# Scores of three attention units in one TensorE block instead of two, with PV written into the unit's own score banks

## Chip, cores and metric

The kernel runs on one core of a Trainium2 chip. The metric is the device time of one launch, in microseconds (us). The engines are TensorE (PE in the profile, with its weight loads as PEld), VectorE (DVE), ScalarE (ACT), GpSimd (POOL) and SyncE (SP). PE writes only into PSUM, which has eight banks; ACT and DVE read it from there.

## What is computed

Sliding-window attention with a linear bias, followed by a feed-forward layer whose gate is h times cos(h):

```python
scores = q @ k.T / sqrt(64)                       # q, k, v: 8 batches, 8 heads, 576 rows, 64 wide
scores = where((rel >= 0) & (rel < 128), scores - slope[h] * rel, -1e9)
x = softmax(scores) @ v                           # brought to 4608 rows x 512
h = x @ w_in                                      # 512 -> 2048
out = (h * cos(h)) @ w_out                        # 2048 -> 512, float32
```

## The kernel before

**Tiling.** The 4608 rows of x are nine chunks of 512 rows (`c` in the main loop). Attention is cut into units of 128 query rows, eight per batch: `units(b)` gives (b, 0, 0), which has all eight heads of the first 128 rows; then for qb = 1, 2, 3 two units each with four heads (hh = 0, 1); then (b, 4, 0), the tail of 64 rows with all eight heads. Because the window is 128 wide, a block of queries needs only its own block of keys and the one before it.

**One unit** goes through these steps:

- scores (L540, matmul in L559): 16 matmuls for the tail, 8 for any other unit. Each uses 64 of PE's 128 rows; the two heads of a pair use the two halves of the rows and write two banks.
- exps (L582): one ACT instruction over both banks (128x1024), from PSUM to the tile `p`.
- mask (L591): one DVE multiplication of `p` by `exp(bias)`, which is 0 outside the window.
- pv (L608): matmuls of `p` with v, 65 columns wide (the 65th is the row sum); 8 matmuls, or 16 for the tail. A unit with qb 0 or 4 is wide and writes both banks 2 and 3; any other writes one of them.
- norm (L648): a DVE reciprocal of the row sum into `rec` and one multiplication, or two for a wide unit, into an SBUF tile.
- the way into `xT`: either a DMA transpose on SP's queue (`x_dma`), or two or four PE transposes and a copy by ACT or DVE (`x_pe`), which use the same bank as the PV.

**Feed-forward.** `moe1(c)` makes for each of 16 column blocks four matmuls 512 wide into one bank (L750), a Sin on ACT (L755) and a product on DVE (L759). `moe2(c)` makes for each of four row blocks 16 matmuls 512 wide (L803), a copy to SBUF by ACT or DVE (L810, L811) and a store on SP.

**Banks.** `SB` = 4 to 7 hold scores, `UB` = 2, 3 hold PV, `OB` = 0, 1 hold moe2's sums. moe1 goes round the banks 2 to 7.

**Order.** The main loop lists for each chunk c: moe1(c), then the attention units that the next chunk needs (phase c: eight units, nine in phase 6), then moe2(c). Before it stands phase -1, seven units. `attention` takes the units two at a time: one block of scores for two units, two exps, two masks, then PV of both together, or one after the other where a wide unit is among them. The listed operations then go through `Plan.schedule`: a list scheduler with a fixed cost for each operation and a priority (norm and the way into xT first, then exps, masks and PV, then scores, moe1, moe2). It writes one fixed order for each engine, and `Plan.emit` sets the semaphore waits. The ACT table allows only Exp of phase c, then Sin of chunk c + 1, and so on in turn. Nothing of the order is decided on the chip; an instruction that is not ready holds up all behind it on its engine.

The first four units of a phase (two in phase 0) go into xT through SP's queue ahead of everything that depends on them: the DMA transposes of the next batch's q and k (L406, L409) stand behind them on SP, and the loads of v on POOL's queue wait for them.

Of the kernel before, what the change touches and what calls it, by code (L numbers as in the profile page):

```python
# [8 lines left out]
F32 = mybir.dt.float32  # L9
BF16 = mybir.dt.bfloat16  # L10
# [274 lines left out]
def bass_alibi_sliding__then__act_gcu_kernel(  # L285
# [8 lines left out]
    with ExitStack() as ctx:  # L294
# [26 lines left out]
        cosb = [sb(f"cos{i}", [128, 512], F32) for i in range(NCOS)]  # L321
        NOB = 4
        ob = [sb(f"ob{i}", [128, 512], F32) for i in range(NOB)]
        rec = [sb(f"rec{i}", [128, 8], F32) for i in range(2)]
        ident = sb("ident", [128, 128])
        zeros = sb("zeros", [128, 128])
        halfpi = sb("halfpi", [128, 1], F32)
# [2 lines left out]

        ps = ctx.enter_context(nc.psum_tensor("ps", [128, 8, 512], F32))
        BPE = 2
        QUOTA = [8, 8, 8, 8, 8, 8, 9]
        BIASED = [(0, 0, 0)] + [(0, qb, hh) for qb in range(1, 3) for hh in range(2)]
        SB, UB, OB = [4, 5, 6, 7], [2, 3], [0, 1]
# [204 lines left out]
        def scores(us, slot):  # L540

            def f(e):
                ins = None
                for n, u in enumerate(us, slot):
                    b, qb, hh = u
                    banks = SB[2 * n:2 * n + 2]
                    acc = u in BIASED
                    if qb == 0:
                        jobs = [(128 * pr, 128, pr, 0) for pr in range(NPAIR)]
                    elif qb == 4:  # L550
                        jobs = [(128 * pr + 64 * i, 64, pr, 3 + i) for pr in range(NPAIR)
                                for i in range(2)]
                    else:
                        jobs = [(256 * i + 128 * j, 128, 2 * hh + i, qb - 1 + j)
                                for i in range(2) for j in range(2)]
                    for n, (c0, n_, pr, kc) in enumerate(jobs):
                        stop = not acc or n == len(jobs) - 1
                        for x in range(2):
                            ins = e.matmul(ps[:, banks[x], c0:c0 + n_], keys_ap(b, x, pr, kc),  # L559
                                           query_ap(b, x, pr, qb, n_), start=not acc, stop=stop)  # L560
                return ins
            keys, held, occ = [], [], 0
            for n, u in enumerate(us, slot):
                keys += tkeys(u)
                held += [("B", x) for x in SB[2 * n:2 * n + 2]]
                occ += 250 if u[1] == 4 else 230
                if u in BIASED:
                    b, qb, hh = u
                    for x in range(2):
                        rhs = BT[:, x, :, 128:256] if qb == 0 else BT[:, x, 2 * hh:2 * hh + 2, :]  # L570
                        prs = range(NPAIR) if qb == 0 else range(2 * hh, 2 * hh + 2)
                        bank = SB[2 * n + x]
                        op("pe", lambda e, rhs=rhs, bank=bank: e.matmul(  # L573
                            ps[:, bank, :], ident[:, :], rhs, start=True, stop=False),
                           r=[("BT", 2 * pr + x) for pr in prs] + ["ident"], w=[("B", bank)],
                           occ=216, lat=379, pri=2)
            op("pe", f, r=keys, w=held, occ=occ, lat=occ + 165, mode=1, pri=2)
# [2 lines left out]
        pbuf = {}  # L580

        def exps(u, n, table):  # L582
            banks = SB[2 * n:2 * n + 2]
            i = pbuf[u] = pcount[0] % NP
            pcount[0] += 1
            op("act", lambda e: e.activation(  # L586
                P[i][:, 0:1024], ps[:, banks[0]:banks[0] + 2, :].rearrange("p a b -> p (a b)"),
                ACTF.Exp, scale=0.125),
               w=[("B", x) for x in banks] + [("P", i)], occ=940, lat=1040, table=table, pri=1)
# [18 lines left out]
        def pv(us):  # L608

            def f(e):  # L610
                ins = None
                for u, ub in us:
                    b, qb, hh = u
                    i, V = pbuf[u], vp[b % 2]
                    if qb in (0, 4):
                        for x in range(2):
                            for k_ in range(NPAIR):
                                h = 2 * k_ + x
                                o = ps[:, UB[x], 65 * k_:65 * k_ + 65]
                                c0 = 512 * x + 128 * k_  # L620
                                ins = e.matmul(o, P[i][:, c0:c0 + 128],  # L621
                                               V[:, 3 if qb else 0, h, 0:65],
                                               start=True, stop=not qb)
                                if qb:
                                    ins = e.matmul(o, P[i][:, c0 + 64:c0 + 192], V[:, 4, h, 0:65],  # L625
                                                   start=False, stop=True)
                        continue
# [11 lines left out]
            for u, ub in us:  # L639
                b, qb, hh = u  # L640
                wide = qb in (0, 4)
                reads += [("P", pbuf[u]), ("vinit", b % 2)]
                reads += [("v", b % 2, t) for t in range(max(0, qb - 1), qb + 1)]
                held += [("B", x) for x in (UB if wide else [ub])]
                occ += 480 if qb == 4 else 240
            op("pe", f, r=reads, w=held, pri=1, occ=occ, lat=occ + 165)

        def norm(u, ub, n):  # L648
            b, qb, hh = u
            rc = rec[n % 2]  # L650
            if qb in (0, 4):
                m = 64 if qb else 128
                xt_ = xtl[b % 2] if qb else xfirst
                key = ("xtl", b % 2) if qb else "xfirst"
                U = ps[0:m, UB[0]:UB[0] + 2, 0:260].rearrange("p x (k c) -> p x k c", c=65)
                rv = rc[0:m, 0:8].rearrange("p (x k) -> p x k", x=2)
                o = xt_[:, :].rearrange("p (k x d) -> p x k d", k=4, x=2)
                op("dve", lambda e: e.reciprocal(rv, U[:, :, :, 64]),
                   w=[("B", UB[0]), ("B", UB[1]), ("rec", n % 2)], occ=120, lat=200, pri=0)
                for x in range(2):  # L660
                    op("dve", lambda e, x=x: e.tensor_tensor(
                        o[:, x, :, :], U[:, x, :, 0:64],
                        rv[:, x, :, None].broadcast_to([m, 4, 64]), ALU.mult),
                       r=[("rec", n % 2)], w=[("B", UB[x]), key], occ=340, lat=420, pri=0)
                return
            U = ps[:, ub, 0:260].rearrange("p (r x c) -> p r x c", r=2, c=65)
            rv = rc[:, 0:4].rearrange("p (r x) -> p r x", r=2)
            key = ("xnat", n % NX)
            o = xnat[n % NX][:, :].rearrange("p (r x d) -> p r x d", r=2, x=2)
            op("dve", lambda e: e.reciprocal(rv, U[:, :, :, 64]),  # L670
               w=[("B", ub), ("rec", n % 2)], occ=100, lat=182, pri=0)
            op("dve", lambda e: e.tensor_tensor(  # L672
                o, U[:, :, :, 0:64], rv[:, :, :, None].broadcast_to([128, 2, 2, 64]), ALU.mult),
               r=[("rec", n % 2)], w=[("B", ub), key], occ=340, lat=425, pri=0)

        def xkeys(prs, t0, n):
            return [("xT", pr, t // 64) for pr in prs for t in range(t0, t0 + n, 64)]
# [1 line left out]
        def x_pe(u, ub, n):  # L679
# [3 lines left out]
            if qb in (0, 4):  # L683
                m = 64 if qb else 128
                xt_ = xtl[b % 2] if qb else xfirst
                rk = [("xtl", b % 2) if qb else "xfirst"]
                half = ps[:, UB[0]:UB[0] + 2, :].bitcast(BF16)[:, :, 768:1024]

                def f(e):
                    ins = None  # L690
# [2 lines left out]
                        ins = e.transpose(half[:, y, c0:c0 + m],  # L693
                                          xt_[:, 128 * k_:128 * k_ + 128], ident[0:m, 0:m])
                    return ins
                banks = UB[0:1] if qb else UB
                op("pe", f, r=rk + ["ident"], w=[("B", x) for x in banks],
                   occ=240, lat=410, pri=0)
                if qb:
                    parts = [(xT[:, :, t0:t0 + 64],  # L700
                              half[:, 0, :].rearrange("p (k t) -> p k t", k=4), every, [UB[0]])]
                else:
                    parts = [(xT[:, 2 * y:2 * y + 2, t0:t0 + 128],
                              half[:, y, :].rearrange("p (k t) -> p k t", k=2),
                              range(2 * y, 2 * y + 2), [UB[y]]) for y in range(2)]
            else:
                dst = ps[:, ub, :].bitcast(BF16)[:, 768:1024]

# [111 lines left out]

        def attention(us, phase):

            begin = []
            for g in range(0, len(us), 2):
                two = us[g:g + 2]
                if phase < 0:
                    for n, u in enumerate(two):
                        scores([u], n)
                        exps(u, n, 0)
                        mask(u)  # L830
                else:
                    scores(two, 0)
                    for n, u in enumerate(two):
                        exps(u, n, 2 * phase + 2)
                    for u in two:
                        mask(u)
                sets = [list(zip(two, UB))]
                if phase < 0 or any(u[1] in (0, 4) for u in two):
                    sets = [[s] for s in sets[0]]
                for set_ in sets:  # L840
                    pv(set_)
                    after = []
                    for u, ub in set_:
                        n = ucount[0]
                        ucount[0] += 1
                        norm(u, ub, n)
                        soon = g < (4 if phase else 2) and phase >= 0
                        after.append((soon, t_first(u) // CH > phase + 1, u, ub, n))
                    for soon, late, u, ub, n in after:
                        if soon:  # L850
# [2 lines left out]
                            x_dma(u, n)  # L853
                        else:
                            x_pe(u, ub, n)
            return begin

        load_qk("q", q, 0, 0)
# [95 lines left out]
```

## Time and profile before

| what | value |
|---|---|
| median of 3 runs | 311.3 us (311.07 to 311.45) |
| the profiled execution | 311.13 us |
| its span, first to last instruction | 309.3 us |
| busy PE, ACT, DVE, POOL | 301.1, 205.6, 189.9, 97.2 us |
| granted PE clock | 1.000 |
| PE matmuls L803, L750 | 130.7 us, 112.4 us |

In a row of the timeline stand the start (us from the start of the span), the time from the start of the first to the end of the last of the merged instructions, the engine, the line, the operation, output and input, and the count. In square brackets stands how long the engine had been idle before it, and what ended that. In the chain of work that ended last, a piece is a start, a length and what ran. Matmuls overlap: one that is shown with 0.38 us is followed by the next after 0.216 us. A few per cent of the matmul records are missing, so a merged row can show one less than ran.

### The profile page before, as it was taken

To read this page: it belongs to the slowest core of one execution; us is meant where nothing else is said; L and a number is where in the kernel's file an instruction comes from. 1 tells how busy PE (TensorE), PEld (TensorE's weight loads), DVE (VectorE), ACT (ScalarE), POOL (GpSimd) and SP (SyncE) were. 2 spreads that over 40 slices of the span, in tenths; PEclk is the share of its full clock that TensorE was granted. 3 is DMA by queue.
4 is the path that set the end of the run, shared out by engine and by line. 5 is a ranking of instruction groups with operands and counts; after the bars stand their busy time and mean duration, and the time that the engine had idled before them with its cause. 6 is when DMAs were issued, how large, how long until landed. Compare 5 with 4: busy or idle time off the path is not lost.

```text
span 309.3 us, 6639 instructions
## 1 busy us (share of the span) xinstructions
PE 301.1 (97%) x2675; PEld 161.4 (52%) x2717; DVE 189.9 (61%) x400; ACT 205.6 (66%) x276; POOL 97.2 (31%) x122
## 2 busy tenths in 40 slices
PE   7899999999999999999999999999999999999996
PEld 5689756445544554455445544454455544444444
DVE  6687667585867586857784777487748880453000
ACT  7797865885787778758777768668668682462211
POOL 8997200582055505550573056405000000000000
PEclk9999999999999999999999999999999999999999
DMA  9999999999499949994999399949923201101112
GB/s 147 172 204 207 207 163 195 184 159 144 77 130 141 194 84 146 131 202 109 151 142 189 89 116 159 194 118 158 117 94 77 45 0 36 68 0 69 69 70 100
DMA packets 150334, 39.09 MB, mean 126 GB/s; under 512 B 138913, under 2 KB 145313, under 8 KB 150305
## 3 DMA queue, kind: packets, MB, share of 16 engines
q0 software_dynamic: 100688, 18.10, 84.1%
q1 hardware_dynamic: 49344, 20.33, 31.7%
q8 instruction: 21, 0.34, 0.5%
q10 hardware_dynamic: 272, 0.26, 0.3%
q14 instruction: 9, 0.07, 0.1%
HBM read 36.70 MB, written 9.44 MB: 149 GB/s over the span
## 4 chain that ended last, share of the span: by engine, by line
PE 96%; issue 1%; DVE 1%; ACT 1%; POOL 0%; ACTq 0%; POOLq 0%
PE ps L803 40%; PE ps L750 35%; PE ps L559 6%; PE ps L775 5%; PE ps L633 2%; PE ps L635 2%; PE ps L500 2%; PE ps L621 2%; PE ps L573 1%; PE ps L712 1%; PE ps L625 1%; DVE gT L759 0%; ACT cos L755 0%; ACT p L586 0%; PE ps L495 0%
## 5 line engine op out<-in xcount | busy, mean ns | idle before, releaser
L803 PE MATMUL ps<-w_outb,gT 128*128 128x512 bf16 (+2 forms) x563 | 130.7, 373 | 2.1 <-issue 1.0
L750 PE MATMUL ps<-xT,w_inb 128*128 128x512 bf16 x501 | 112.4, 379 | 0.6
L759 DVE TENSOR_TENSOR gT<-ps,cos 128x512 bf16<-128x512 f32 x128 | 86.0, 689 | 38.4 <-ACT cos L755 22.0
L755 ACT ACTIVATE cos<-ps,halfpi 128x512 f32<-128x512 f32 x128 | 85.7, 687 | 25.9 <-PE ps L750 17.9
L803 PEld LDWEIGHTS ps<-w_outb,gT 128*128 128x128 bf16 x592 | 53.4, 98 | 56.8 <-DVE ob L811 0.2
L750 PEld LDWEIGHTS ps<-xT,w_inb 128*128 128x128 bf16 x512 | 49.5, 98 | 59.2 <-issue 1.1
L586 ACT ACTIVATE p<-ps 128x1024 bf16<-128x1024 f32 x64 | 62.1, 1021 | 27.1 <-PE ps L559 26.8
L386 POOL DMA_DIRECT2D vp<-in_v_dram x40 | 33.9, 870 | 84.8 <-DMA xT<-xnat 63.4
L605 DVE TENSOR_TENSOR p<-p,emask 128x1024 bf16<-128x1024 bf16 x59 | 40.0, 685 | 21.3 <-ACT p L586 21.3
L810 ACT ACTIVATE ob<-ps 128x512 f32<-128x512 f32 (+2 forms) x26 | 15.1, 581 | 38.5 <-PE ps L803 38.4
L397 POOL DMA_DIRECT2D qnat<-in_q_dram x30 | 25.3, 872 | 19.1 <-DMA qt<-qnat 19.1
L397 POOL DMA_DIRECT2D knat<-in_k_dram x30 | 25.4, 878 | 11.8 <-DMA kt<-knat 10.1
L559 PE MATMUL ps<-qt,kt 64*128 64x128 bf16 (+1 forms) x576 | 20.8, 213 | 0.3 <-DVE kt L516 0.3
L559 PEld LDWEIGHTS ps<-qt,kt 64*128 64x128 bf16 x576 | 14.7, 95 | 10.9 <-ACT p L586 5.5
L672 DVE TENSOR_TENSOR xnat<-ps,rec 128x256 bf16<-128x256 f32 x48 | 18.3, 419 | 0.2
L775 PE MATMUL ps<-xT,w_inb 128*128 128x128 bf16 x256 | 16.4, 219 | 0.0
L633 PEld LDWEIGHTS ps<-vp,p 128*128 128x128 bf16 x192 | 13.0, 97 | 6.1 <-issue 5.9
L633 PE MATMUL ps<-vp,p 128*128 128x65 bf16 x192 | 15.0, 193 | 0.2 <-DVE xT L722 0.2
L635 PE MATMUL ps<-vp,p 128*128 128x65 bf16 x192 | 15.1, 193 | 0.0
L775 PEld LDWEIGHTS ps<-xT,w_inb 128*128 128x128 bf16 x256 | 14.6, 98 | 0.7
L635 PEld LDWEIGHTS ps<-vp,p 128*128 128x128 bf16 x192 | 12.5, 97 | 0.1
L811 DVE COPY ob<-ps 128x512 f32<-128x512 f32 x11 | 7.5, 682 | 8.1 <-PE ps L803 8.1
(66 smaller groups left out, 157.3 us busy)
## 6 DMA issues: line engine op xcount, KB each, us to landing
out_dram<-ob SPq DMA_DIRECT2D x35, 256.0 KB, 3.2
vp<-in_v_dram POOLq DMA_DIRECT2D x32, 128.0 KB, 6.6
qnat<-in_q_dram POOLq DMA_DIRECT2D x24, 128.0 KB, 6.9
knat<-in_k_dram POOLq DMA_DIRECT2D x24, 128.0 KB, 5.4
w_outb<-in_moe_w_out_dram POOLq DMA_DIRECT2D x4, 512.0 KB, 21.1
w_inb<-in_moe_w_in_dram POOLq DMA_DIRECT2D x3, 512.0 KB, 11.1
qrows<-in_q_dram POOLq DMA_DIRECT2D x1, 576.0 KB, 14.4
krows<-in_k_dram POOLq DMA_DIRECT2D x1, 576.0 KB, 16.8
```

The source lines that it names most:

```text
L386: op("pool", [lambda e, t=t, rows=rows: e.dma_start(vp[b % 2][0:rows, t, :, 0:64], v[b, :, 128 * t:128 * t + rows, :].rearrange("h p d -> ...
L397: fns.append(lambda e, t=t, rows=rows: e.dma_start(nat[which][0:rows, t, :, :], src[b, :, 128 * t:128 * t + rows, :].rearrange("h p d -> p ...
L559: ins = e.matmul(ps[:, banks[x], c0:c0 + n_], keys_ap(b, x, pr, kc), query_ap(b, x, pr, qb, n_), start=not acc, stop=stop)
L586: op("act", lambda e: e.activation(P[i][:, 0:1024], ps[:, banks[0]:banks[0] + 2, :].rearrange("p a b -> p (a b)"), ACTF.Exp, scale=0.125), ...
L605: op("dve", lambda e: e.tensor_tensor(p, p, m, ALU.mult), r=[("P", i), ("EM", 0), ("EM", 1)], w=[("P", i)], occ=600, lat=690, pri=1)
L633: e.matmul(o, P[i][:, c0:c0 + 128], V[:, qb - 1, h, 0:65], start=True, stop=False)
L635: ins = e.matmul(o, P[i][:, c0 + 128:c0 + 256], V[:, qb, h, 0:65], start=False, stop=True)
L750: op("pe", lambda e, kc=kc: e.matmul(ps[:, bank, :], w_in[:, kc, 128 * fc:128 * fc + 128], xT[:, kc, r0:r0 + CH], start=(kc == 0), stop=(k ...
L755: op("act", lambda e: e.activation(cosb[ci][:, :], ps[:, bank, :], ACTF.Sin, bias=halfpi[:, 0:1]), r=["halfpi"], w=[("B", bank), ("cos", c ...
L759: op("dve", lambda e: e.tensor_tensor(gT[gi][:, fc, :], ps[:, bank, :], cosb[ci][:, :], ALU.mult), r=[("cos", ci)], w=[("B", bank)] + [("g ...
L775: ins = e.matmul(ps[:, bank, 128 * i:128 * i + 128], w_in[:, kc, 128 * fc:128 * fc + 128], xT[:, kc, t0:t0 + 128], start=(kc == 0), stop=( ...
L803: op("pe", lambda e, t=t, fc=fc, bank=bank, j0=j0, j1=j1: e.matmul(ps[:, bank, 0:j1 - j0], gT[gi][:, fc, 128 * t:128 * t + 128], w_out[:, ...
```

## The change

From phase 1 on the units are grouped by three: 3, 3, 2 in phases 1 to 5, and 3, 3, 3 in phase 6. The scores of a group are one block on PE. Unit n of a group has the banks 4 and 5, 6 and 7, or 2 and 3 (`SLOT`), for its scores, its PV and its transposes. Each unit's mask, PV and norm are listed unit by unit. Phases -1 and 0 stay in groups of two with the old banks. There are four `rec` tiles instead of two.

```diff
-        rec = [sb(f"rec{i}", [128, 8], F32) for i in range(2)]
+        rec = [sb(f"rec{i}", [128, 8], F32) for i in range(4)]
...
+        GROUPS = [[2] * 4] + [[3, 3, 2]] * 5 + [[3] * 3]
+        SLOT = [4, 6, 2]
@@ scores @@
-                    banks = SB[2 * n:2 * n + 2]
+                    banks = [SLOT[n], SLOT[n] + 1]
@@ exps @@
-            banks = SB[2 * n:2 * n + 2]
+            banks = [SLOT[n], SLOT[n] + 1]
@@ pv, the wide unit @@
-                                o = ps[:, UB[x], 65 * k_:65 * k_ + 65]
+                                o = ps[:, ub + x, 65 * k_:65 * k_ + 65]
...
-                held += [("B", x) for x in (UB if wide else [ub])]
+                held += [("B", x) for x in ([ub, ub + 1] if wide else [ub])]
@@ attention @@
-            begin = []
-            for g in range(0, len(us), 2):
-                two = us[g:g + 2]
+            begin, g = [], 0
+            sizes = ([[2] * 4] + GROUPS + [[], []])[phase + 1]
+            own = 3 in sizes
+            for many in sizes:
+                some = us[g:g + many]
                 if phase < 0:
...
                 else:
-                    scores(two, 0)
-                    for n, u in enumerate(two):
+                    scores(some, 0)
+                    for n, u in enumerate(some):
                         exps(u, n, 2 * phase + 2)
-                    for u in two:
+                if not own:
+                    outs = [UB[0] if u[1] in (0, 4) else UB[n] for n, u in enumerate(some)]
+                    for u in some if phase >= 0 else []:
                         mask(u)
-                sets = [list(zip(two, UB))]
-                if phase < 0 or any(u[1] in (0, 4) for u in two):
-                    sets = [[s] for s in sets[0]]
+                    sets = [list(zip(some, outs))]
+                    if phase < 0 or any(u[1] in (0, 4) for u in some):
+                        sets = [[x] for x in sets[0]]
+                else:
+                    sets = [[x] for x in zip(some, SLOT)]
                 for set_ in sets:
+                    if own:
+                        mask(set_[0][0])
                     pv(set_)
...
-                        soon = g < (4 if phase else 2) and phase >= 0
+                        soon = us.index(u) < (4 if phase else 2) and phase >= 0
...
+                g += many
```

The norm and the transposes of a wide unit follow the same exchange, from `UB[0]`, `UB[1]` to `ub`, `ub + 1`.

More of the change, by code (lines that the diff above doesn't have):

```diff
@@ L564, in scores @@
                 keys += tkeys(u)
-                held += [("B", x) for x in SB[2 * n:2 * n + 2]]
+                held += [("B", SLOT[n] + x) for x in range(2)]
                 occ += 250 if u[1] == 4 else 230
@@ L571, in scores @@
                         prs = range(NPAIR) if qb == 0 else range(2 * hh, 2 * hh + 2)
-                        bank = SB[2 * n + x]
+                        bank = SLOT[n] + x
                         op("pe", lambda e, rhs=rhs, bank=bank: e.matmul(
@@ L649, in norm @@
             b, qb, hh = u
-            rc = rec[n % 2]
+            rc = rec[n % 4]
             if qb in (0, 4):
@@ L654, in norm @@
                 key = ("xtl", b % 2) if qb else "xfirst"
-                U = ps[0:m, UB[0]:UB[0] + 2, 0:260].rearrange("p x (k c) -> p x k c", c=65)
+                U = ps[0:m, ub:ub + 2, 0:260].rearrange("p x (k c) -> p x k c", c=65)
                 rv = rc[0:m, 0:8].rearrange("p (x k) -> p x k", x=2)
@@ L658, in norm @@
                 op("dve", lambda e: e.reciprocal(rv, U[:, :, :, 64]),
-                   w=[("B", UB[0]), ("B", UB[1]), ("rec", n % 2)], occ=120, lat=200, pri=0)
+                   w=[("B", ub), ("B", ub + 1), ("rec", n % 4)], occ=120, lat=200, pri=0)
                 for x in range(2):
@@ L663, in norm @@
                         rv[:, x, :, None].broadcast_to([m, 4, 64]), ALU.mult),
-                       r=[("rec", n % 2)], w=[("B", UB[x]), key], occ=340, lat=420, pri=0)
+                       r=[("rec", n % 4)], w=[("B", ub + x), key], occ=340, lat=420, pri=0)
                 return
@@ L670, in norm @@
             op("dve", lambda e: e.reciprocal(rv, U[:, :, :, 64]),
-               w=[("B", ub), ("rec", n % 2)], occ=100, lat=182, pri=0)
+               w=[("B", ub), ("rec", n % 4)], occ=100, lat=182, pri=0)
             op("dve", lambda e: e.tensor_tensor(
                 o, U[:, :, :, 0:64], rv[:, :, :, None].broadcast_to([128, 2, 2, 64]), ALU.mult),
-               r=[("rec", n % 2)], w=[("B", ub), key], occ=340, lat=425, pri=0)
+               r=[("rec", n % 4)], w=[("B", ub), key], occ=340, lat=425, pri=0)
         def xkeys(prs, t0, n):
@@ L686, in x_pe @@
                 rk = [("xtl", b % 2) if qb else "xfirst"]
-                half = ps[:, UB[0]:UB[0] + 2, :].bitcast(BF16)[:, :, 768:1024]
+                half = ps[:, ub:ub + 2, :].bitcast(BF16)[:, :, 768:1024]
                 def f(e):
@@ L695, in f @@
                     return ins
-                banks = UB[0:1] if qb else UB
+                banks = [ub] if qb else [ub, ub + 1]
                 op("pe", f, r=rk + ["ident"], w=[("B", x) for x in banks],
@@ L700, in x_pe @@
                     parts = [(xT[:, :, t0:t0 + 64],
-                              half[:, 0, :].rearrange("p (k t) -> p k t", k=4), every, [UB[0]])]
+                              half[:, 0, :].rearrange("p (k t) -> p k t", k=4), every, [ub])]
                 else:
@@ L704, in x_pe @@
                               half[:, y, :].rearrange("p (k t) -> p k t", k=2),
-                              range(2 * y, 2 * y + 2), [UB[y]]) for y in range(2)]
+                              range(2 * y, 2 * y + 2), [ub + y]) for y in range(2)]
             else:
@@ L831, in attention @@
                 else:
-                    scores(two, 0)
-                    for n, u in enumerate(two):
+                    scores(some, 0)
+                    for n, u in enumerate(some):
                         exps(u, n, 2 * phase + 2)
-                    for u in two:
+                if not own:
+                    outs = [UB[0] if u[1] in (0, 4) else UB[n] for n, u in enumerate(some)]
+                    for u in some if phase >= 0 else []:
                         mask(u)
-                sets = [list(zip(two, UB))]
-                if phase < 0 or any(u[1] in (0, 4) for u in two):
-                    sets = [[s] for s in sets[0]]
+                    sets = [list(zip(some, outs))]
[3 more added lines that the diff above has]
+                    sets = [[x] for x in zip(some, SLOT)]
                 for set_ in sets:
+                    if own:
+                        mask(set_[0][0])
                     pv(set_)
```

## Prediction

> **What bounds the kernel now.** I read the page first: busy shares, the slices, the chain that ended last.
>
> ```profile
> span 309.3 us, 6639 instructions
> ...
> PE 301.1 (97%) x2675; PEld 161.4 (52%) x2717; DVE 189.9 (61%) x400; ACT 205.6 (66%) x276; POOL 97.2 (31%) x122
> ...
> PE   7899999999999999999999999999999999999996
> ...
> PEclk9999999999999999999999999999999999999999
> ...
> PE 96%; issue 1%; DVE 1%; ACT 1%; POOL 0%; ACTq 0%; POOLq 0%
> PE ps L803 40%; PE ps L750 35%; PE ps L559 6%; PE ps L775 5%; PE ps L633 2%; PE ps L635 2%; PE ps L500 2%; PE ps L621 2%; PE ps L573 1%; PE ps L712 1%; PE ps L625 1%; DVE gT L759 0%; ACT cos L755 0%; ACT p L586 0%; PE ps L495 0%
> ```
>
> PE is 97% busy in the span, at full clock in every slice, and is 96% of the chain. In phases 1 to 6, which the change touches, it should then be possible to add up PE's time alone: what goes from its queue goes from the end. The chain in order of time gives the beat of the long matmuls.
>
> ```profile
> 54.80 8.20 PE ps L750 x38
> ```
>
> 8.20 / 38 = 0.216 us for each 512-wide matmul. Next PE's timeline around two attention blocks, first one in the middle of a phase, then one from the start of the kernel, where a score block holds one unit.
>
> ```profile
> 107.73 0.59 PE L803 MATMUL ps<-w_outb,gT 128*128 128x512 bf16 x2
> 108.22 0.40 PE L621 MATMUL ps<-vp,p 128*128 128x65 bf16 x8
> 108.46 0.81 PE L803 MATMUL ps<-w_outb,gT 128*128 128x512 bf16 x3
> 109.20 0.62 PE L559 MATMUL ps<-qt,kt 64*128 64x128 bf16 x16
> 109.75 0.39 PE L803 MATMUL ps<-w_outb,gT 128*128 128x512 bf16 x1
> ```
>
> ```profile
> 15.94 0.19 PE L635 MATMUL ps<-vp,p 128*128 128x65 bf16 x1
> 16.07 0.40 PE L559 MATMUL ps<-qt,kt 64*128 64x128 bf16 x8
> 16.40 0.29 PE L775 MATMUL ps<-xT,w_inb 128*128 128x128 bf16 x2
> ```
>
> **What a score block costs beyond its matmuls.** *In:* the three matmuls from 108.46 fill the queue to 108.46 + 3 x 0.216 = 109.11, but the scores start at 109.20: 0.09 us. After a PV matmul it is 15.94 to 16.07, that is 0.13 where PV matmuls follow each other after 0.03 (below): 0.10. *Out:* from the start of the scores to the next kind it is 0.55 us for two units (109.20 to 109.75) and 0.33 for one (16.07 to 16.40). A unit therefore costs 0.22, and 0.33 - 0.22 = 0.11 is left that doesn't depend on the number of units. In and out together: 0.20 us for each block. The rows are rounded to 0.01, so 0.18 to 0.22.
>
> **What a PV block costs beyond its matmuls.** The eight PV matmuls at 108.22 are followed by L803 at 108.46: 0.24, or 0.03 each, with nothing left over. They enter 108.22 - (107.73 + 2 x 0.216) = 0.06 late, which is a wait. So cutting PV of two units into two blocks costs nothing in itself, only what a new wait may cost.
>
> **The change, part by part.**
>
> *Score blocks removed.* In the built order PE has 35 score blocks before and 28 after: in phases 1 to 5 three instead of four, in phase 6 three instead of five. Their 576 score matmuls are the same, as are PE's other counts (592 of L803, 768 of moe1, 576 of PV, 36 transposes). Saved: 7 x 0.20 = **1.4 us** (1.26 to 1.54).
>
> *PV split.* PV blocks go from 43 to 61. By the rows above: 0.
>
> *Masks unit by unit, four rec tiles.* Both are DVE matters; rec is written and read on DVE alone, so PE's path gains nothing by it: 0.
>
> *Work moved from ACT to DVE.* Five output copies and one copy into xT change sides in the built order.
>
> ```profile
> L810 ACT ACTIVATE ob<-ps 128x512 f32<-128x512 f32 (+2 forms) x26 | 15.1, 581 | 38.5 <-PE ps L803 38.4
> L811 DVE COPY ob<-ps 128x512 f32<-128x512 f32 x11 | 7.5, 682 | 8.1 <-PE ps L803 8.1
> L722 DVE COPY xT<-ps 128x256 bf16<-128x256 bf16 x9 | 2.4, 286 | 0.3 <-PE ps L712 0.2
> ```
>
> DVE gets 5 x 0.68 + 0.29 = 3.7 us over six phases, at 61% busy. PE's matmuls hide it; where the cover is gone it costs what the next part bounds.
>
> *New waits.* A group now holds all six banks 2 to 7. The next group's scores must wait for the norm of the third unit, where before they waited only for two exps. I walk the second group of a phase from the start of its scores, with these rows:
>
> ```profile
> 109.86 1.94 ACT L586 ACTIVATE p<-ps 128x1024 bf16<-128x1024 f32 x2 [0.96 <-PE ps L559]
> ```
>
> ```profile
> 110.92 0.69 DVE L605 TENSOR_TENSOR p<-p,emask 128x1024 bf16<-128x1024 bf16 x1 [0.66 <-ACT p L586]
> ```
>
> The first exp starts 109.86 - 109.20 = 0.66 after two units' scores, so 0.88 after three. Two exps take 1.94 and one alone 1.02 (L586 mean in the groups, quoted below), so the second adds 0.92. The mask starts 110.92 - (109.86 + 1.02) = 0.04 after the exp and takes 0.69. The first PV may start at 0.88 + 1.02 + 0.04 + 0.69 = 2.63, plus some 0.1 from an ACT copy's end to PE:
>
> ```profile
> 84.98 0.71 ACT L721 ACTIVATE xT<-ps 128x256 bf16<-128x256 bf16 x2 [0.43 <-PE ps L712]
> ```
>
> ```profile
> 85.79 0.19 PE L633 MATMUL ps<-vp,p 128*128 128x65 bf16 x1
> ```
>
> (84.98 + 0.71 = 85.69, and the PV that waited starts at 85.79.) That is 2.73. In the built order nine 512-wide matmuls stand between these scores and this PV: 0.55 + 0.22 + 9 x 0.216 = 2.71. It is a tie, within the rounding. The third group, of two units, gives 0.66 + 1.02 + 0.04 + 0.69 + 0.1 = 2.51 against 0.55 + 1.94 = 2.49, the same tie. So there are 12 places (two a phase) where PV stands just where its mask ends. The first group has 15 such matmuls, 1.3 us more, and spare time. The next score block needs the third unit's norm, so I walk the first group too:
>
> ```profile
> 163.25 0.63 PE L559 MATMUL ps<-qt,kt 64*128 64x64 bf16 x24
> 163.81 1.47 PE L803 MATMUL ps<-w_outb,gT 128*128 128x512 bf16 x5
> ```
>
> ```profile
> L672 DVE TENSOR_TENSOR xnat<-ps,rec 128x256 bf16<-128x256 f32 x48 | 18.3, 419 | 0.2
> L670 DVE RECIPROCAL rec<-ps 128x4 f32<-128x4 f32 x48 | 6.1, 166 | 7.2 <-PE ps L635 7.0
> ```
>
> Scores of tail and first block leave after 0.56, with a third unit after 0.78. Then the built order has 15 matmuls (3.24), the tail's PV (16 x 0.03 = 0.48), 3 matmuls (0.65), PV (0.24), 4 (0.86), PV (0.24), 7 (1.51), and the next scores 0.09 later: 8.1 us behind the group's start. The last PV ends at 6.5; reciprocal and multiplication (0.17 and 0.42, some 0.1 before each) end at 7.3 if DVE is free, and some 7.7 with another multiplication ahead: 0.4 spare. A PV or score block that comes late holds up all of PE's queue behind it: moe2's matmuls, the next scores, and with them ACT's exps.
>
> What the waits cost is therefore bounded by: below, the waits that go (PV of the wide first unit waited for the tail's norm in banks 2 and 3, the 0.06 above, once in each of six phases: -0.4); above, 0.1 late at each of 12 places: +1.2. I take 0, since before also loses such 0.06s and the nearest row (0.06) makes 12 x 0.06 - 0.4 = +0.3 at most.
>
> *DMA.* POOL's order is unchanged. On SP the fourth early unit's transpose now stands behind two stores.
>
> ```profile
> 71.35 0.63 PE L559 MATMUL ps<-qt,kt 64*128 64x64 bf16 x24
> ```
>
> ```profile
> 83.50 1.24 SPq L737 DMA_TRANSPOSE xT<-xnat  x1
> ...
> 86.46 0.89 POOL L386 DMA_DIRECT2D vp<-in_v_dram  x1 [15.00 <-DMA xT<-xnat]
> ```
>
> ```profile
> 100.83 2.64 POOL L397 DMA_DIRECT2D knat<-in_k_dram  x3 [2.77 <-DMA kt<-knat]
> ```
>
> ```profile
> 101.91 0.63 PE L559 MATMUL ps<-qt,kt 64*128 64x64 bf16 x24
> ```
>
> It lands at most 2.96 us after its issue (83.50 to 86.46). In the new order its PV is the first of the second group, 10.8 us (8.1 + 2.7) behind the phase's first scores, which stand at 71.35, and so at 82.2; the norm takes about 1 us, so the issue is at some 83.2, not later than before. The k transposes behind it on SP ended by 100.83, 1.1 us ahead of their scores at 101.91. I cost both at 0; that cover is 1.1 us a phase.
>
> *Sum.* 311.13 - 1.4 + 0 = 309.7 for the profiled execution (span 309.3 and 1.8 around it). The median of the runs, 311.3, stands 0.17 above it: 309.9.
>
> **The rivals.**
>
> *The waits eat the saving.* Each of the 12 tied PVs comes 0.1 late: -1.4 + 1.2 gives 311.1. For it: 12 ties, no slack. Against it: before waits for masks and copies too, and the profile puts only single idle times on PE's matmuls in these phases:
>
> ```profile
> PE ps L803 <- issue: 1.0, 6, 0.2
> PE ps L633 <- DVE xT L722: 0.2, 1, 0.2
> ```
>
> *Emptying the banks becomes the bound; slower.* DVE is in order, and one of its other instructions may stand ahead of a mask at a tied PV. Here it happened:
>
> ```profile
> 105.77 0.69 DVE L811 COPY ob<-ps 128x512 f32<-128x512 f32 x1 [0.47 <-PE ps L803]
> 106.38 0.68 DVE L605 TENSOR_TENSOR p<-p,emask 128x1024 bf16<-128x1024 bf16 x1
> ```
>
> The mask began 0.61 after the copy. If that happens at half of the 12 places, and PE has nothing to cover it, it costs 6 x 0.6 = 3.6: 311.3 - 1.4 + 3.6 = 313.5. It decides from (1.4 + 0.6) / 12 = 0.17 late on average. Against it: the built order has the mask of a tied PV ahead of the copies, and ACT and DVE have room in the phase:
>
> ```profile
> L586 ACT ACTIVATE p<-ps 128x1024 bf16<-128x1024 f32 x64 | 62.1, 1021 | 27.1 <-PE ps L559 26.8
> L605 DVE TENSOR_TENSOR p<-p,emask 128x1024 bf16<-128x1024 bf16 x59 | 40.0, 685 | 21.3 <-ACT p L586 21.3
> ```
>
> ACT's exps waited 26.8 us in total for scores, so they are fed by PE and not the reverse. The Trainium skill, "TensorEngine Tiling (Array Packing)", section "PSUM Bottleneck", speaks for this rival: tiling makes TensorE faster but not the emptying of PSUM, and the copies out of PSUM may become the bottleneck. By that rule the sum would be this rival's; the trace of before doesn't bear it out, with the 26.8 us of exps waiting for scores.
>
> *More than the switches.* The waits on the tail's norm go and no new ones come: 309.9 - 0.4 = 309.5.
>
> *The change doesn't do what it says.* The built order has the 28 blocks; no chance for it.
>
> **How the numbers follow.** About 0.2% (0.6 us) is what a measurement of this kernel can tell from no change: faster is below 310.7, slower above 311.9. Forecast 309.9, chance 0.72, with 309.4 to 310.6 as its own range; more than the switches (309.5) 0.06; waits eat it (311.1) 0.14, of which 0.02 below 310.7; DVE as the bound (313.5) 0.08. So faster 0.80, same 0.12, slower 0.08. Range: 309.2 (7 x 0.22 and the 0.4 of waits, rounded out) to 311.1, which leaves out the slower rival and half of the tied one.
>
> **What would show it.** Phases 1 to 5 each shorter by 0.20 on PE and phase 6 by 0.40; a score block of three units at 0.77 from its start to the next kind; PV blocks that follow the 0.216 beat without gaps; score blocks 28. Wrong would be: PV or scores that start over 0.1 late at the tied places, with a mask or a norm that ended just before; a gap before moe1's first matmuls (the xT transposes); or the k transposes ending after their scores' turn.

## The result, and the profile after

| | before | after |
|---|---|---|
| median | 311.13 us | 310.31 us |
| ratio, with 95% interval | | 0.9974 (0.9962 to 0.9986) |
| span of the profiled execution | 309.3 us | 308.4 us |

0.8 us less, where 1.4 were forecast; the interval is 0.4 to 1.2 us. The page of after, for the lines shown of before (busy shares, clock, chain):

```profile
PE 299.3 (97%) x2675; PEld 161.4 (52%) x2717; DVE 193.7 (63%) x406; ACT 201.4 (65%) x270; POOL 97.0 (31%) x122
...
PEclk9999999999999999999999999999999999999999
...
PE 90%; DMA 3%; POOL 2%; ACT 2%; issue 1%; DVE 1%; POOLq 0%; ACTq 0%
```

PE is still 97% busy at full clock, with 1.8 us less busy time, so the bound is the same. What is new in the chain, DMA and POOL, belongs to the start. PE's own waits there show it:

```profile
PE ps L778 <- DMA w_inb<-in_moe_w_in_dram: 0.7, 1, 0.7
```

In this execution the first blocks of moe1 waited 0.7 us for w_in. Ahead of phase 1 both kernels have PE's instructions in the same order, so I split the time there: a **start**, up to the first score block of phase 1, and a **stretch**, from there to the end of the last matmul. For each kernel that takes one row of PE's timeline and the last row of the chain in order of time. Before (its first row is in the prediction), then after:

```profile
297.19 9.71 PE ps L803 x60
```

```profile
71.72 0.85 PE L562 MATMUL ps<-qt,kt 64*128 64x64 bf16 x32
```

```profile
294.55 11.44 PE ps L806 x68
```

Before: 297.19 + 9.71 - 71.35 = 235.55. After: 294.55 + 11.44 - 71.72 = 234.27. The stretch is 1.28 us shorter and the start 0.37 longer. (In the expectations the stretch goes to the start of the last matmul and is 0.23 to 0.24 shorter.) All kernels of this study, by the same rows of their own traces. Each ratio is to runs of before made beside the kernel; their medians are 311.13 to 311.23 us:

| kernel | start | stretch | median | ratio to before (95%) |
|---|---|---|---|---|
| before, three profiles | 71.35, 71.35, 70.80 | 235.55, 235.57, 235.58 | 311.13 | |
| after, three profiles | 71.72, 71.08, 72.75 | 234.27, 234.29, 234.29 | 310.31 | 0.9974 (0.9962 to 0.9986) |
| pv_later, two profiles | 71.14, 71.09 | 233.79, 233.78 | 309.26, 309.4 | 0.9944 (0.9928 to 0.996), 0.9935 (0.9921 to 0.995) |
| split_scores | 71.89 | 238.41 | 313.43 | 1.0077 (1.0062 to 1.0092) |
| two_rot | 71.52 | 236.01 | 312.1 | 1.0027 (1.0013 to 1.0042) |
| pv_sooner | 71.15 | 238.88 | 314.32 | 1.0093 (1.0077 to 1.0109) |
| two_own | 71.36 | 245.72 | 321.31 | 1.0322 (1.0302 to 1.0343) |

The stretch repeats within 0.03 us, while the start lies anywhere from 70.80 to 72.75 us, with the same order on the engines up to there.

**Time outside the span.** The medians differ by 0.8 us and the stretches by 1.28. Most of the rest lies neither in the start nor in the stretch. A run's time is longer than its span (first to last instruction, recorded to 0.1 us), and by how much is on record:

| kernel | runs with a recorded span | time less span | median span |
|---|---|---|---|
| before | 33 | 1.75 to 1.85 us | 309.4 us |
| after | 39 | 2.08 to 2.17 us | 308.1 us |

After loses 0.3 us outside of its span in every run, and the median spans are 1.3 us apart, as the stretches are. What makes these 0.3 us isn't shown: no row of a profile lies outside the span. two_rot loses them too (2.12 to 2.21 us), the other four kernels of the table don't (1.76 to 1.87).

**A place that was forecast as a tie.** PE's timeline of after, second group of phase 1: scores, the matmuls behind them, the last two of these, and the first PV with what follows it.

```profile
79.85 0.84 PE L562 MATMUL ps<-qt,kt 64*128 64x128 bf16 x24
80.62 2.12 PE L806 MATMUL ps<-w_outb,gT 128*128 128x512 bf16 x9
...
82.14 0.59 PE L806 MATMUL ps<-w_outb,gT 128*128 128x512 bf16 x2
82.63 0.19 PE L636 MATMUL ps<-vp,p 128*128 128x65 bf16 x1
...
82.86 0.38 PE L806 MATMUL ps<-w_outb,gT 128*128 128x512 bf16 x1
```

And DVE's, around it:

```profile
78.98 0.41 DVE L675 TENSOR_TENSOR xnat<-ps,rec 128x256 bf16<-128x256 f32 x1
81.79 0.69 DVE L608 TENSOR_TENSOR p<-p,emask 128x1024 bf16<-128x1024 bf16 x1 [2.40 <-ACT p L589]
```

A block of three units leaves 80.62 - 79.85 = 0.77 after its start, as worked out. The norm that these scores needed ended at 78.98 + 0.41 = 79.39, 0.46 ahead of them (0.4 was worked out). The mask ends at 81.79 + 0.69 = 82.48. PE had free space from 82.14 + 2 x 0.216 = 82.57, but PV starts at 82.63: 0.06 late, and 0.15 after the mask's end.

I measured every gap between two matmul starts in the stretch against the beat of its kind (0.216, or 0.03 in PV, and the entries and exits of score blocks). Beyond the beat are 0.48 us before and 0.73 after; ten of the 12 tied PVs are 0.05 late. At all 14 places of after where a PV waits for its mask, it starts 0.15 us behind the mask's end. No score block is late: each starts 0.09 to 0.10 beyond the beat, as the price of a block has it. With 7 x 0.203 = 1.42 us of removed blocks, 0.25 more waits, and 0.11 less in gaps of 0.01, that makes -1.28: the whole difference of the stretch. Why there are fewer gaps of 0.01 isn't shown.

### The profile page after: what moved, and what is told of

Read it like the earlier page. It is cut to its first block, busy times and chain, and to the rows that moved or that the text cites. A ratio compares the mean times of both kernels' runs of the same rounds, so it can differ in the third digit from the quotient of the medians.

```text
span 308.4 us, 6651 instructions
## 1 busy us (share of the span) xinstructions
PE 299.3 (97%) x2675; PEld 161.4 (52%) x2717; DVE 193.7 (63%) x406; ACT 201.4 (65%) x270; POOL 97.0 (31%) x122
## 4 chain that ended last, share of the span: by engine, by line
PE 90%; DMA 3%; POOL 2%; ACT 2%; issue 1%; DVE 1%; POOLq 0%; ACTq 0%
PE ps L806 38%; PE ps L753 36%; PE ps L562 5%; PE ps L778 5%; DMA w_inb<-in_moe_w_in_dram 3%; ACT p L589 2%; PE ps L636 2%; PE ps L638 2%; PE ps L624 1%; PE ps L503 1%; POOL vp L389 1%; PE ps L628 1%; DVE p L608 1%; PE ps L715 1%; POOL qrows L381 0%
## 5 line engine op out<-in xcount | busy, mean ns | idle before, releaser
L806 PE MATMUL ps<-w_outb,gT 128*128 128x512 bf16 (+2 forms) x565 | 132.2, 373 | 2.2 <-issue 1.1
L753 PE MATMUL ps<-xT,w_inb 128*128 128x512 bf16 x499 | 113.9, 379 | 0.7
L762 DVE TENSOR_TENSOR gT<-ps,cos 128x512 bf16<-128x512 f32 x128 | 85.0, 687 | 19.5 <-ACT cos L758 14.6
L758 ACT ACTIVATE cos<-ps,halfpi 128x512 f32<-128x512 f32 x128 | 84.7, 688 | 17.9 <-PE ps L753 13.9
L813 ACT ACTIVATE ob<-ps 128x512 f32<-128x512 f32 (+2 forms) x21 | 12.1, 577 | 41.3 <-PE ps L806 34.7
L675 DVE TENSOR_TENSOR xnat<-ps,rec 128x256 bf16<-128x256 f32 x48 | 19.9, 421 | 1.4
L814 DVE COPY ob<-ps 128x512 f32<-128x512 f32 x16 | 10.9, 684 | 15.5 <-PE ps L806 15.5
L562 PE MATMUL ps<-qt,kt 64*128 64x128 bf16 (+1 forms) x576 | 19.2, 211 | 0.6 <-DVE kt L519 0.6
L636 PEld LDWEIGHTS ps<-vp,p 128*128 128x128 bf16 x192 | 14.2, 97 | 8.9 <-issue 6.3
L636 PE MATMUL ps<-vp,p 128*128 128x65 bf16 x192 | 17.4, 193 | 0.2 <-DVE xT L725 0.2
L638 PE MATMUL ps<-vp,p 128*128 128x65 bf16 x192 | 17.5, 193 | 0.0
L638 PEld LDWEIGHTS ps<-vp,p 128*128 128x128 bf16 x192 | 13.2, 97 | 2.3
```

What stands on the lines that cost most here:

```text
L636: e.matmul(o, P[i][:, c0:c0 + 128], V[:, qb - 1, h, 0:65], start=True, stop=False)
L638: ins = e.matmul(o, P[i][:, c0 + 128:c0 + 256], V[:, qb, h, 0:65], start=False, stop=True)
L753: op("pe", lambda e, kc=kc: e.matmul(ps[:, bank, :], w_in[:, kc, 128 * fc:128 * fc + 128], xT[:, kc, r0:r0 + CH], start=(kc == 0), stop=(k ...
L758: op("act", lambda e: e.activation(cosb[ci][:, :], ps[:, bank, :], ACTF.Sin, bias=halfpi[:, 0:1]), r=["halfpi"], w=[("B", bank), ("cos", c ...
L762: op("dve", lambda e: e.tensor_tensor(gT[gi][:, fc, :], ps[:, bank, :], cosb[ci][:, :], ALU.mult), r=[("cos", ci)], w=[("B", bank)] + [("g ...
L806: op("pe", lambda e, t=t, fc=fc, bank=bank, j0=j0, j1=j1: e.matmul(ps[:, bank, 0:j1 - j0], gT[gi][:, fc, 128 * t:128 * t + 128], w_out[:, ...
```

## The experiments

**The start: the same kernels again.** No edit.

> The changed kernel once more, to see what of the time lies ahead of the change. Up to the first score block of phase 1 both kernels have the same order on every engine; in the first profiles that block started at 71.35 us before and 71.72 after, where PE waited 0.73 us for a piece of w_in. From there to the last matmul it was 235.31 before and 234.04 after. Theory: the stretch from that block to the end repeats within 0.1 us (234.0), and the start moves by some tenths from run to run. Rival: the later start belongs to the changed kernel and is there again (71.7).

> The kernel before once more, for a profile: whether its stretch from the first scores of phase 1 to the last matmul repeats (235.31 us) and how far its start moves. Theory: the stretch repeats within 0.1 us, and the first scores of phase 1 stand anywhere from 71 to 73 us as in the profiles of the changed kernels, which have the same order up to there. Rival: before starts early each time (71.3), so that the changed kernel's start is later by itself.

> The same a third time: 235.31 us for the stretch; the start between 71 and 73 us by the theory, 71.3 by the rival.

> The changed kernel beside pv_later_2 on the same chip: 234.04 us from the first scores of phase 1 to the last matmul, 0.4% less than before by that stretch (1.27 us), and a start that differs by some tenths of a us.

after_again gave a ratio of 0.9961 (0.9946 to 0.9975), after_3 again 0.9974 (0.9961 to 0.9988). The stretches came out as said (table). The starts: before 71.35, 71.35 and 70.80, after 71.72, 71.08 and 72.75, the other changed kernels 71.09 to 71.89. So the start of after isn't late each time, and it wasn't 71.3 for before each time; 70.80 also lies below the 71 to 73 that the theory gave. In these few profiles the changed kernels' starts lie higher on average. The recorded spans of all runs don't bear that out: their medians differ by as much as the stretches, which leaves nothing clear of the scatter for the start.

**PV one matmul later.** The scheduler's cost for a mask, from phase 1 on:

```diff
-               r=[("P", i), ("EM", 0), ("EM", 1)], w=[("P", i)], occ=600, lat=690, pri=1)
+               r=[("P", i), ("EM", 0), ("EM", 1)], w=[("P", i)], occ=600,
+               lat=740 if (b, qb) >= (1, 4) else 690, pri=1)
```

> In the after kernel the scheduler is told that a mask of phases 1 to 6 takes 50 ns longer, so that it puts ten long matmuls instead of nine between the scores of a second or third group and the first PV. Theory: the 12 PVs that came about 0.05 us late are on time then, 0.4 to 0.6 us less than after (309.8), and their wait is gone from the timeline; one matmul of moe1 in phase 1 may wait 0.14. Rival: the late PVs are covered or their wait only moves to the next scores: same as after.

> pv_later once more beside after, for the size of its gain: 233.56 us from the first scores of phase 1 to the last matmul, as in its first profile, 0.48 less than after; 0.5% less than before.

The place of above in pv_later's timelines of PE and DVE:

```profile
81.78 0.59 PE L807 MATMUL ps<-w_outb,gT 128*128 128x512 bf16 x2
82.21 0.19 PE L637 MATMUL ps<-vp,p 128*128 128x65 bf16 x1
```

```profile
81.20 0.69 DVE L608 TENSOR_TENSOR p<-p,emask 128x1024 bf16<-128x1024 bf16 x1 [2.18 <-ACT p L589]
```

PV starts at 81.78 + 2 x 0.216 = 82.21, on the beat; the mask had ended at 81.89, 0.32 earlier. The gaps beyond the beat fall from 0.73 to 0.16, and the stretch by 0.48 to 0.51, twice. The late PVs had cost what they showed, ten times 0.05. One matmul of moe1 in phase 1 now waits 0.10. pv_later is faster than before by 0.6% and has a shorter stretch than after by 0.5 us; of the 0.7 to 1.2 us between its medians and those of after made beside it, 0.3 lie outside the span.

**PV one matmul sooner.** The same line with `lat=500`.

> The opposite of pv_later: the scheduler is told that a mask of phases 1 to 6 takes 190 ns less than in after, so that it puts eight long matmuls instead of nine between the scores of a second or third group and the first PV. Theory (PE is in order and nothing covers a late PV): each of the 12 PVs is late by 0.05 + 0.22 = 0.27 us, 12 x 0.22 = 2.6 us more than after in the stretch from phase 1 to the end (236.6 instead of 234.0), which turns the gain into a loss: 312.5. Rival (PE makes up for it later): within 0.5 us of after.

```profile
81.60 0.59 PE L807 MATMUL ps<-w_outb,gT 128*128 128x512 bf16 x2
82.30 0.19 PE L637 MATMUL ps<-vp,p 128*128 128x65 bf16 x1
```

```profile
81.46 0.69 DVE L608 TENSOR_TENSOR p<-p,emask 128x1024 bf16<-128x1024 bf16 x1 [2.27 <-ACT p L589]
```

PE was free at 82.03 and the PV came at 82.30: 0.27 late, as expected, and again 0.15 after the mask's end (82.15). Eleven of the 12 tied PVs are late by this much, and the theory holds for them. The total is larger than I expected, 4.6 us instead of 2.6: the scheduler also moved other PVs forward, of which four in first groups are 0.20 late and three more 0.19 to 0.24. And moe1 waits 0.40 in phase 1 for a transpose into xT; the twelfth tied PV stands behind that wait and is on time. All gaps beyond the beat are 4.6 us more than in after, the whole difference, so PE made up for none of them.

**More score blocks, nothing else.** The third unit's scores in a block of their own:

```diff
-                    scores(some, 0)
+                    scores(some[:2], 0)
                     for n, u in enumerate(some):
-                        exps(u, n, 2 * phase + 2)
+                        if n == 2:
+                            scores([u], 2, [first])
+                        first = exps(u, n, 2 * phase + 2) if n == 0 else exps(u, n, 2 * phase + 2) and first
```

(`scores` hands the list to its operation as `after`; `exps` returns its operation.)

> The after kernel with the third unit's scores of each group in a block of their own, behind the group's first exp: 40 score blocks instead of 27, all banks and groups as after. Theory (each block costs 0.20 us of mode change): 13 x 0.20 = 2.6 us more than after, 312.9. Rival (the saving comes from PV in the score banks and its other waits, not from the number of blocks): within 0.5 us of after, 310.3 to 310.8.

The stretch is 4.1 us longer than after, not 2.6. Most of what is on top lies at the first matmuls of moe1 in phases 1 and 2. In phase 1:

```profile
87.79 0.82 PE L753 MATMUL ps<-xT,w_inb 128*128 128x512 bf16 x3 [0.59 <-DMA xT<-xnat]
```

There PE waited for the transpose of the fourth early unit into xT. It was not issued later than in after, but 0.9 us earlier (83.27; in after 84.19), as moe1 too began 0.9 earlier (86.16; 87.05). It took longer to land: 4.5 us from its issue, in after 3.0. In phase 2 it was 4.1 us against 2.7. Why it took longer isn't shown. Matmul starts show 0.76 and 0.31 us beyond the beat at the two places. All gaps beyond the beat are 1.4 us more than in after, and those of 0.01 are 0.14. That leaves 4.1 - 1.4 - 0.14 = 2.6 for 13 blocks, 0.20 each. The price of a block holds; that the split has no other cost was wrong. (The median is only 3.1 above that of after, since this kernel doesn't lose the 0.3 outside its span and the starts scatter.)

**PV in the score banks, with groups of two.**

```diff
-        GROUPS = [[2] * 4] + [[3, 3, 2]] * 5 + [[3] * 3]
+        GROUPS = [[2] * 4] * 6 + [[2] * 4 + [1]]
...
-            own = 3 in sizes
+            own = phase > 0
...
-                    scores(some, 0)
-                    for n, u in enumerate(some):
+                    scores(some, g if own else 0)
+                    for n, u in enumerate(some, g if own else 0):
...
-                    sets = [[x] for x in zip(some, SLOT)]
+                    sets = [[(u, SLOT[n % 3])] for n, u in enumerate(some, g)]
```

(and `SLOT[n % 3]` for `SLOT[n]` in scores and exps)

> The after kernel with groups of two from phase 1 on; the units take the three pairs of banks in turn, PV stays in the banks of its own unit's scores. 34 score blocks as before. Theory (blocks make the time, the new place of PV nothing): 7 x 0.20 = 1.4 us more than after, that is before's time give or take 0.4 (311.1). Rival (the new place of PV makes the gain): the time of after, 310.3.

The median, 312.1, is 0.9 above that of before beside it, more than the 0.4 that the theory allowed; some 0.35 of it lie outside the span. The stretch is 236.01: 1.74 more than after and 0.46 more than before. The gaps beyond the beat are 0.93 (before 0.48), which is the 0.46. So with as many blocks as before, the new place of PV gives no gain of its own; it costs half a microsecond of waits.

**The same without turning the banks.** Only the first two edits of two_rot, so that a group always has banks 4 to 7.

> The after kernel with groups of two that always take banks 4 to 7, with PV in the banks of its own unit's scores; banks 2 and 3 serve moe1 alone. 34 score blocks as before. The next scores then wait for the norm of both units of the group before. By the rows of before a group lasts some 5 us from scores to scores (the exps end at 2.6, the second PV at some 4.3, its norm 0.7 later), four groups 20 us in a phase in which moe2 has 13.8 us of matmuls for PE, scores and PV 5 and moe1 some 1.7 in banks 2 and 3. Theory: the emptying of the banks sets the time of these phases, and PE stands idle on norms by 1 to 2 us a phase: 6 to 12 us more than before, 317 to 323. Rival (new place of PV costs nothing in any grouping): before's time with the waits of two_rot, 311 to 312.

10.2 us more than before in the stretch, inside what was expected. PE's groups, with the idle time ahead of them and what ended it:

```profile
L753 PE MATMUL ps<-xT,w_inb 128*128 128x512 bf16 x499 | 114.5, 379 | 4.6 <-ACT p L589 1.7 <-DVE xtail L664 1.0 <-ACT xT L724 0.6
L636 PE MATMUL ps<-vp,p 128*128 128x65 bf16 x192 | 17.4, 193 | 2.9 <-ACT p L589 1.5 <-DVE p L608 1.1 <-DVE xT L725 0.2
```

It isn't the norms alone that PE waits for, as I had written, but the whole way out of the banks: in these two rows exps end 3.2 us of the idle time, masks 1.1, the tail's norm 1.0, the copies into xT 0.8. moe2's matmuls are used up before the last groups are through (in phase 1 at 85.9 us, and PV then waits until 87.51), and PE has nothing to put there. This is the slower rival of the prediction, in a kernel that has fewer banks for it. The Trainium skill, "TensorEngine Tiling (Array Packing)", section "PSUM Bottleneck", says that tiling doesn't speed up the emptying of PSUM, and that the copy out of it may become the bottleneck after a fourfold speedup of TensorE. two_own shows such a bound, 10.2 us, but by banks that come free later and not by a faster TensorE; after doesn't show it, since none of its score blocks is late.

## Why the prediction was right, and where its sizes were off

- **PE's queue is the bound: right.** The stretch can be added up from matmul starts to 0.01 us in after, before and two_rot.
- **0.20 us for each score block: right.** 7 blocks make 1.42 us in after, and 13 blocks 2.6 in split_scores, once the waits are taken off. (PE's score blocks are 34 and 27 on the trace and its PV blocks 42 and 60; the prediction counted one more of each in both, where two early blocks stand back to back.)
- **PV in more blocks costs nothing by itself: right.** Eight PV matmuls take 82.86 - 82.63 = 0.23 in a block of their own.
- **What the waits cost, taken as 0: too small.** It is +0.25, between the bounds of -0.4 and +1.2. The 12 ties were found, and ten of them are 0.05 late. Two sizes were off. The step from the end of a mask to PE was taken as 0.1 from an ACT copy, and it is 0.15 from DVE's mask (82.48 to 82.63, 82.15 to 82.30), which makes the ties late. And the wait for the tail's norm that goes, 0.06, was counted in each of six phases (-0.4), but before shows it in two only, at 108.22 and 231.70 us: -0.12. Before also has PVs that wait for their mask, one of them 0.16 late at 167.21.
- **Scores wait for the third unit's norm, 0.4 spare: right** (0.46).
- **The 1.8 us around the span, carried over unchanged: too small.** It is 2.1 in every run of after. These 0.3 are the larger part of what the median misses: -1.28 in the stretch and +0.3 outside the span leave about -1.0, of which -0.8 was measured. Nothing in the profile of before could have told it.
- **Early transposes and copies moved to DVE cost nothing: right in after**, which has no wait for xT. But the walk there was off: the fourth transpose is issued at 84.19, not at 83.2, and the 2.96 taken as the most that a transpose needs to land is passed in split_scores (4.5 us), where PE waits for it.
- **The sign that phases 1 to 5 would each be shorter by 0.20: wrong.** From the first scores of phase 1 to those of phase 2 it is 30.6 us before and 31.9 after, since the new order has more long matmuls ahead of the second place (262 matmuls in this window of before, 269 in that of after). A schedule that moves work over a phase's edge can't be checked phase by phase; only the whole stretch can.
- **The rivals.** The waits ate 0.25 of the saving, not 1.2. Emptying the banks didn't become the bound in after. "More than the switches" is out, since the waits grew.
- **Open:** what makes the 0.3 us outside the span, and why there are fewer gaps of 0.01. About 0.1 of the 0.46 between the medians' difference and the stretch's is left to the scatter of the starts.

## What to carry to other kernels

Where PE's queue is the path, count how often it changes between matmuls on 64 and on 128 of its rows: each visit to the 64-row ones cost 0.20 us here whatever it held, so grouping pays by visits, and only as long as the group's banks are emptied before the next visit. Then look for ties: a fixed order that places a consumer on the very matmul at which its input ends loses a few hundredths at each, and one matmul more ahead of it (pv_later) gives them back, while one less costs its whole length. And compare two kernels from a point up to which both do the same, since a start that depends on loads can scatter more than the change is worth, and look at what a run takes outside its span: here 0.3 us of 1.3 were lost there.

## What the runs showed of the hardware

From the end of DVE's mask to the start of the PV that waits for it took 0.15 us at all 14 such places of after's stretch; from the end of an ACT copy it was 0.10 (85.69 to 85.79, before). A block of 64-row score matmuls cost 0.20 us beyond its matmuls, by 7 blocks fewer (after) and by 13 more (split_scores). The fourth transpose of phase 1 into xT took 3.0 us to land in after and 4.5 in split_scores. And the stretch of 234 to 236 us repeated within 0.03 us in three profiles each of before and after, while its start moved between 70.80 and 72.75.
